# Small-window attention on quarters of the TensorE array: two heads and two query halves side by side, in place of block-diagonal k and v

## The chip, the cores and the metric

The kernel runs on one core of one Trainium2 chip. The metric is the device time of one execution in microseconds (us). The kernel before took 328.46 us in the median of four runs beside the changed one (326.58 to 329.01).

## The reference, cut to what matters

Batch 8, 8 heads, 576 positions, head dimension 64. Each head has two attentions whose results are added: a down-sampled one over 144 groups of four positions, and a local one in which position i sees only positions less than 4 away. A GELU layer pair (512 to 2048 to 512) follows on all 4608 tokens.

```python
q_d = q.reshape(B, H, Sd, 4, D).mean(axis=3)          # the same for k_d, v_d
out_d = softmax(scale * q_d @ k_d.T) @ v_d
mask = abs(pos[:, None] - pos[None, :]) < 4
out_local = softmax(where(mask, scale * q @ k.T, -1e9)) @ v
x = repeat(out_d, 4) + out_local                        # [B, H, S, D], then tokens x 512
out = gelu(x @ w_in) @ w_out
```

## The kernel before: the parts that matter

Batch 0 has its own attention and is not changed. Batches 1 to 7 run their attention between the matmuls of the two projections: `fill(n)` puts n projection matmuls (128x128 array, 512 columns each) between the steps, so that TensorE has work while ScalarE (ACT) and VectorE (DVE) compute exponentials and products. One step treats a pair of heads, p. With a head dimension of 64, two heads share the 128 rows of the array; k and v of a window are laid out block-diagonal, with zeros off the diagonal, so that each head meets only its own keys.

```python
def scores(b, p):                       # 10 windows of 57 or 60 queries, block-diagonal kb
    for hh in range(2):
        matmul(sc[:, 512*hh+SH : 512*hh+SH+Sd], lhsT=kdz[:, p, hh, 0:128], rhs=qd[:, p, :])
    for j in range(NW):
        matmul(sc[:, c : c+QL[j]], lhsT=kb[:, p, j, :], rhs=q[:, p, QN[j] : QN[j]+QL[j]])
    ...                                 # ACT: two Exp, ed (down-sampled) and e (local)

def av(b, p):
    for g in range(2):                  # sums of e, by a block matrix of ones
        matmul(sc[:, 512*g : 512*g+SH], lhsT=ON2, rhs=e[:, SH*g : SH*g+SH])
    for hh in range(2):                 # down-sampled: v and sums in one 128-column weight
        matmul(o, lhsT=vd[:, 2*p+hh, :], rhs=ed[:, hh, :], start=True, stop=False)
        matmul(o, lhsT=vlm[:, 2*p+hh, :], rhs=eL, start=False, stop=True)
    for j in range(NW):                 # windows, block-diagonal v
        matmul(nm[:, c : c+QL[j]], lhsT=vw[:, j, p, :], rhs=e[:, QN[j] : QN[j]+QL[j]])

def norm_out(b, p):                     # ACT: 1/sum as exp(-ln(sum)), local and down-sampled apart
    Ln(lr2 <- sc);  Exp(lr2);  Ln(lrd <- nm[64:128]);  Exp(lrd)
    ...                                 # DVE: xl = nm*lr2, up = nm*lrd (per head), xT = xl + up

def attn(b, fill):
    ...
    for p in range(NP):
        if p + 1 < NP: scores(b, p + 1); mask(p + 1); fill(2)
        else:          fill(4)
        av(b, p); norm_out(b, p)
        if p + 1 < NP: fill(9)
```

(Arguments shortened; sc has two buffers of two PSUM banks, nm has one.)

The softmax here doesn't subtract the row's maximum and nothing guards it: scores larger than these inputs give would overflow.

## Time and profile before

| | |
|---|---|
| time, median | 328.46 us |
| TensorE busy in the profiled execution | 317.1 of 324.5 us |
| one batch, from the third on | 32.70 us |
| of it projections: 128 matmuls of 512 columns at 0.216 | 27.65 us |
| of it attention | 5.05 us |

One batch is the distance between two starts of the first projection's first matmuls, in the chain that ended last (134.80 and 167.50, for example; read to the nanosecond in the trace, it is 32.70 in each of the five). The views that carry this are in the prediction. One more belongs here, because the change merges them: the four ACT groups of a pair's reciprocals, from the view of groups, with count, busy us and mean ns of one.

```profile
L427 ACT ACTIVATE lr<-lr 128x576 f32<-128x576 f32 x28 | 19.1, 683 | 0.9
L426 ACT ACTIVATE lr<-sc 128x576 f32<-128x576 f32 x28 | 18.4, 658 | 0.0
L429 ACT ACTIVATE lr<-lr 64x288 f32<-64x288 f32 x28 | 12.4, 443 | 0.9
L428 ACT ACTIVATE lr<-nm 64x288 f32<-64x288 f32 x28 | 11.4, 407 | 0.7
```

Together 2.19 us a pair, 61 us of ACT in all.

### The profile page before, as it was taken

To read this page: it belongs to the slowest core of one execution; us is meant where nothing else is said; L and a number is where in the kernel's file an instruction comes from. 1 tells how busy PE (TensorE), PEld (TensorE's weight loads), DVE (VectorE), ACT (ScalarE), POOL (GpSimd) and SP (SyncE) were. 2 spreads that over 40 slices of the span, in tenths; PEclk is the share of its full clock that TensorE was granted. 3 is DMA by queue.
4 is the path that set the end of the run, shared out by engine and by line. 5 is a ranking of instruction groups with operands and counts; after the bars stand their busy time and mean duration, and the time that the engine had idled before them with its cause. 6 is when DMAs were issued, how large, how long until landed. Compare 5 with 4: busy or idle time off the path is not lost.

```text
span 324.5 us, 6382 instructions
## 1 busy us (share of the span) xinstructions
PE 317.1 (98%) x2562; PEld 171.8 (53%) x2562; DVE 190.2 (59%) x410; ACT 226.7 (70%) x401; POOL 121.1 (37%) x152
## 2 busy tenths in 40 slices
PE   8899999999999999999999999999999999999995
PEld 4775556555554455445544554455445544444444
DVE  6787676667588917891789778927791750000001
ACT  8787558865887688768877787778777877415610
POOL 8965858969285155455077106200000000000000
PEclk9999999999999999999999999999999999999999
DMA  6999999999999999999999997920200020020011
GB/s 77 162 204 157 161 184 163 173 188 114 169 146 186 186 145 172 202 185 134 172 187 159 169 126 119 149 58 34 97 0 2 34 91 7 2 96 34 0 67 65
DMA packets 150974, 38.76 MB, mean 119 GB/s; under 512 B 132897, under 2 KB 146465, under 8 KB 150945
## 3 DMA queue, kind: packets, MB, share of 16 engines
q0 software_dynamic: 122256, 23.02, 90.4%
q1 hardware_dynamic: 28688, 15.34, 22.8%
q8 instruction: 20, 0.33, 0.4%
q14 instruction: 10, 0.07, 0.1%
HBM read 46.01 MB, written 15.34 MB: 189 GB/s over the span
## 4 chain that ended last, share of the span: by engine, by line
PE 92%; DMA 2%; ACT 2%; POOL 1%; DVE 1%; issue 0%; POOLq 0%; DVEq 0%
PE m_ps L282 36%; PE m_ps L251 33%; PE m_first L241 5%; PE sc L389 2%; PE nm L417 2%; DMA q_nat<-in_q_dram 2%; PE sc L407 2%; PE sc L385 1%; PE m_ps L273 1%; PE nm L413 1%; PE nm L414 1%; PE m_ps L263 1%; POOL k_nat L169 1%; PE tg_k L316 1%; PE tg_q L316 1%; PE sl L373 1%
## 5 line engine op out<-in xcount | busy, mean ns | idle before, releaser
L282 PE MATMUL m_ps<-w_out_sb,gT 128*128 128x512 f16 x544 | 127.6, 379 | 0.0
L251 PE MATMUL m_ps<-xT,w_in_sb 128*128 128x512 f16 x504 | 113.2, 379 | 0.1
L254 ACT ACTIVATE gT<-m_ps 128x512 f16<-128x512 f32 x126 | 75.2, 597 | 37.7 <-PE m_ps L251 37.7
L251 PEld LDWEIGHTS <-w_in_sb 128*128 128x128 f16 x504 | 47.9, 97 | 56.3 <-issue 1.5
L282 PEld LDWEIGHTS <-gT 128*128 128x128 f16 x544 | 49.6, 97 | 52.0 <-issue 0.3
L133 POOL DMA_DIRECT2D v_win<-in_v_dram x56 | 43.5, 812 | 29.9 <-DMA v_grp<-in_v_dram 14.8
L432 DVE TENSOR_TENSOR xl<-nm,lr 128x576 f16<-128x576 f32 x28 | 21.2, 757 | 25.4 <-ACT lr L428 25.4
L277 DVE COPY out_sb<-m_ps 128x256 f32<-128x256 f32 x2 | 0.8, 424 | 54.8 <-PE m_ps L273 54.8
L401 DVE TENSOR_TENSOR e<-e,band 128x576 f16<-128x576 f16 x28 | 12.7, 453 | 30.7 <-ACT e L396 30.7
L286 ACT COPY out_sb<-m_ps 128x512 f32<-128x512 f32 x21 | 12.3, 586 | 25.1 <-PE m_ps L282 24.9
L138 POOL DMA_DIRECT2D v_win<-in_v_dram x14 | 9.8, 787 | 34.6 <-PE nm L417 33.4
L444 DVE TENSOR_TENSOR xT<-xl,up 128x576 f16<-128x576 f16 (+8 forms) x41 | 22.1, 566 | 1.0
L427 ACT ACTIVATE lr<-lr 128x576 f32<-128x576 f32 x28 | 19.1, 683 | 0.9
L395 ACT ACTIVATE ed<-sc 128x288 f16<-128x288 f32 x28 | 11.4, 405 | 10.3 <-PE sc L389 10.3
L426 ACT ACTIVATE lr<-sc 128x576 f32<-128x576 f32 x28 | 18.4, 658 | 0.0
L396 ACT ACTIVATE e<-sc 128x576 f16<-128x576 f32 x28 | 18.0, 644 | 0.0
L434 DVE TENSOR_TENSOR up<-nm,lr 64x144 f16<-64x144 f32 x56 | 16.5, 295 | 0.4
L241 PE MATMUL m_first<-xT,w_in_sb 128*128 128x512 f16 x68 | 16.3, 379 | 0.0
L246 ACT ACTIVATE gT<-m_first 128x1024 f16<-128x1024 f32 x8 | 8.2, 1024 | 8.7 <-PE m_first L241 8.7
L156 POOL DMA_DIRECT2D q<-in_q_dram x5 | 13.8, 2766 | 0.0
L429 ACT ACTIVATE lr<-lr 64x288 f32<-64x288 f32 x28 | 12.4, 443 | 0.9
L307 DVE TENSOR_REDUCE qd<-q_nat 128x576 f16<-128x2304 f16 x5 | 12.8, 2553 | 0.2
(192 smaller groups left out, 467.8 us busy)
## 6 DMA issues: line engine op xcount, KB each, us to landing
out_dram<-out_sb SPq DMA_DIRECT2D x35, 256.0 KB, 2.7
v_win<-in_v_dram POOLq DMA_DIRECT2D x56, 72.0 KB, 7.5
v_grp<-in_v_dram POOLq DMA_DIRECT2D x7, 512.0 KB, 12.7
k<-in_k_dram POOLq DMA_DIRECT2D x5, 576.0 KB, 12.5
q<-in_q_dram POOLq DMA_DIRECT2D x5, 576.0 KB, 14.9
w_in_sb<-in_moe_w_in_dram POOLq DMA_DIRECT2D x4, 512.0 KB, 9.0
w_out_sb<-in_moe_w_out_dram POOLq DMA_DIRECT2D x4, 512.0 KB, 8.3
k_nat<-in_k_dram POOLq DMA_DIRECT2D x12, 96.0 KB, 7.4
```

What stands on the lines that cost most here:

```text
L133: nc.gpsimd.dma_start(out=vw[64 * hh:64 * hh + 64, 0:9, p, 64 * hh:64 * hh + 64], in_=bass.AP(x.tensor, x.offset, [[D, 64], [57 * D, 9], [ ...
L156: nc.gpsimd.dma_start(out=t, in_=src[b].rearrange("h s d -> s h d"))
L241: nc.tensor.matmul(out=half[j], lhsT=w_in_sb[:, fc, 128 * j:128 * j + 128], rhs=xT[:, fc, x0:x0 + 512], start=(fc == 0), stop=(fc == 3))
L251: nc.tensor.matmul(out=ps, lhsT=w_in_sb[:, fc, 128 * j:128 * j + 128], rhs=xT[:, fc, x0:x0 + 512], start=(fc == 0), stop=(fc == 3))
L254: nc.scalar.activation(out=g[:, j, :], in_=ps, func=ACTF.Gelu)
L282: nc.tensor.matmul(out=ps, lhsT=g[:, j, 128 * t:128 * t + 128], rhs=w_out_sb[:, j, :], start=(j == 0), stop=(j == NJ - 1))
L396: nc.scalar.activation(out=e.rearrange("p (g c) -> p g c", g=2), in_=sc2[:, :, 0:SH], func=ACTF.Exp, scale=0.125)
L426: nc.scalar.activation(out=lr2, in_=sc2[:, :, 0:SH], func=ACTF.Ln)
L427: nc.scalar.activation(out=lr2, in_=lr2, func=ACTF.Exp, scale=-1.0)
L432: nc.vector.tensor_tensor(out=xl.rearrange("p (g c) -> p g c", g=2), in0=nm2[:, :, 0:SH], in1=lr2, op=ALU.mult)
L434: nc.vector.tensor_tensor(out=up[64 * hh:64 * hh + 64, :], in0=nm2[0:64, hh, SH:SH + Sd], in1=lrd[:, Sd * hh:Sd * hh + Sd], op=ALU.mult)
L444: nc.vector.tensor_tensor(out=xT[:, p, y:y + z - a].rearrange("p (g r) -> p g r", r=4), in0=xl[:, a:z].rearrange("p (g r) -> p g r", r=4), ...
```

## The change

The intent: a 64-row, 64-column quarter of the array is just one head's window, so four quarters can work at once on two heads and two halves of the queries. The windows multiply and store no blocks of zeros, k needs no copy into blocks, and the sums land so that one Ln and one Exp serve both attentions.

```diff
+    def quad(fn):                       # 5 windows x 2 x 2 quarters
+        for i in range(5):
+            for a in range(2):
+                for c in range(2):
+                    fn(i, a, slice(64*a, 64*a+64), c, slice(64*c, 64*c+64), QO[i], QL[i])
     def scores(b, p):
-            matmul(sc[..], lhsT=kdz[:, p, hh, 0:128], rhs=qd[:, p, :])          # 128x128
+            matmul(sc[..], lhsT=kd[r, p, 0:128], rhs=qd[r, p, :])               # 64x128
-        for j in range(NW): ...                                                 # 10 of 128x128
+        quad(one)                                                               # 20 of 64x64
     def av(b, p):
-        for g in range(2): ... lhsT=ON2 ...                                     # 2 of 288 columns
+        for g in range(2):
+            for hh in range(2):
+                matmul(sc[hs[hh], ..SH], lhsT=ones[hs[g], :], rhs=e[hs[g], hh, :])   # 64x64
-        for hh in range(2): vd, vlm                                             # 4 of 144 columns
+        for o, own, lo in ((sc, None, m4), (nm, L["vd"], L["vlm"])):
+            for g in range(2):
+                for hh in range(2):
+                    matmul(o[hs[hh], c:c+DH], lhsT=fours or own[..], rhs=ed[:, hh, x])   # 128x64
+                matmul(o[:, c:c+DH], lhsT=lo[:, 2*p:2*p+2, :], rhs=eL[:, x])             # 128x128
-        for j in range(NW): ... lhsT=vw ...                                     # 10 of 128x128
+        quad(one)                                                               # 20 of 64x64
     def norm_out(b, p):
-        Ln, Exp on 576 columns; Ln, Exp on 288 columns of 64 partitions; up in two halves
+        Ln, Exp on 720 columns; up in one
     # v windows of batch 1: were loaded head pair by head pair, each between loads of w_out
+    # are loaded window by window, each for all eight heads
     # fills 6, 6, 2, 9, 4 become 5, 6, 2, 10, 3; warm() at the start becomes four more spins
```

(The diff is cut to its core; copies into block form and their tiles go away, and the end-of-sequence scores become four 128x32 matmuls.)

More of the change, by code (lines that the diff above doesn't have):

```diff
@@ L45 @@
     NW = 10
-    WN = [57 * i for i in range(9)] + [512]
-    QN = [0] + [57 * i + 3 for i in range(1, 10)]
-    QL = [60] + [57] * 8 + [60]
+    QL = [58, 58, 58, 57, 57]
+    QO = [0, 58, 116, 174, 231]
+    WN = [[0, 55, 113, 171, 228], [285, 343, 401, 459, 512]]
     SH = S // 2
+    DH = Sd // 2
     cpool = ctx.enter_context(tc.tile_pool(name="const", bufs=1, space=bass.MemoryType.SB))
@@ L61 @@
     I128 = cpool.tile([128, 128], F16, tag="I128", name="I128")
-    band = cpool.tile([128, S], F16, tag="band", name="band")
+    band = cpool.tile([128, 2, SH], F16, tag="band", name="band")
     BH = cpool.tile([128, 64], F16, tag="BH", name="BH")
-    ON2 = cpool.tile([128, 128], F16, tag="ON2", name="ON2")
+    ones = cpool.tile([128, 64], F16, tag="ones", name="ones")
+    fours = cpool.tile([128, 64], F16, tag="fours", name="fours")
+    m4 = cpool.tile([128, H, 64], F16, tag="m4", name="m_four")
     maskL = cpool.tile([128, H], F16, tag="maskL", name="maskL")
@@ L69 @@
     qT0 = cpool.tile([128, NP, S], F16, tag="qT", name="qT")
-    kdt = cpool.tile([128, NP, Sd], F16, tag="kdt", name="kdt")
+    kT0 = cpool.tile([128, NP, S], F16, tag="kT", name="kT")
+    kd = cpool.tile([128, NP, Sd], F16, tag="kd", name="kd")
+    KS = cpool.tile([128, NP, 32], F16, tag="KS", name="KS")
     qd = cpool.tile([128, NP, Sd], F16, tag="qd", name="qd")
-    kb = cpool.tile([128, NP, NW, 128], F16, tag="kb", name="kb")
     kdz = cpool.tile([128, NP, 2, Sd], F16, tag="kdz", name="kdz")
@@ L79 @@
             "kn": ipool.tile([128, 4096], F16, tag="kn", name="k_nat"),
-            "vw": ipool.tile([128, NW, NP, 128], F16, tag="vw", name="v_win"),
+            "vw": ipool.tile([128, 5, H, 64], F16, tag="vw", name="v_win"),
             "vt": ipool.tile([128, H, 4, 64], F16, tag="vt", name="v_grp"),
             "vl": ipool.tile([128, 4, 64], F16, tag="vl", name="v_lo"),
-            "vd": ipool.tile([128, H, 128], F16, tag="vd", name="v_d"),
+            "vd": ipool.tile([128, H, 64], F16, tag="vd", name="v_d"),
             "vls": ipool.tile([128, 64], F16, tag="vls", name="v_ls"),
-            "vlm": ipool.tile([128, H, 128], F16, tag="vlm", name="v_lm"),
+            "vlm": ipool.tile([128, H, 64], F16, tag="vlm", name="v_lm"),
         })
@@ L93 @@
     GL = cpool.tile([128, 8, 16], F16, tag="GL", name="GL")
-    four = cpool.tile([128, H], F32, tag="four", name="four")
     dum = cpool.tile([128, 2], F32, tag="dum", name="dum")
@@ L126, in load_qk, with vw_load @@
                 yield
-    def vw_load(b, src, ps=None):
-        vw = ld[b % 2]["vw"]
-        for p in ps or range(NP):
-            for hh in range(2):
-                x = src[2 * p + hh, 0:64, :]
-                nc.gpsimd.dma_start(out=vw[64 * hh:64 * hh + 64, 0:9, p, 64 * hh:64 * hh + 64],
-                                    in_=bass.AP(x.tensor, x.offset, [[D, 64], [57 * D, 9], [1, D]]))
-    def vw_last(b, src):
-        for hh in range(2):
-            nc.gpsimd.dma_start(out=ld[b % 2]["vw"][64 * hh:64 * hh + 64, 9, :, 64 * hh:64 * hh + 64],
-                                in_=src[hh:H:2, 512:576, :].rearrange("h s d -> s h d"))
+    def vw_load(b, src, i):
+        for g in range(2):
+            w = WN[g][i]
+            nc.gpsimd.dma_start(out=ld[b % 2]["vw"][64 * g:64 * g + 64, i, :, :],
+                                in_=src[:, w:w + 64, :].rearrange("h s d -> s h d"))
     def vg_load(b, src):
@@ L180 @@
     nc.scalar.activation(out=dum[:, 1:2], in_=dum[:, 0:1], func=ACTF.Exp)
-    for t in (kb.rearrange("p a j c -> p (a j c)"), ld[1]["vw"].rearrange("p j a d -> p (j a d)")):
-        nc.scalar.copy(out=t.bitcast(F32).rearrange("p (n c) -> p n c", c=256),
-                       in_=zt.bitcast(F32).unsqueeze(1).broadcast_to([128, 10, 256]))
-    nc.vector.memset(four, 4.0)
+    nc.vector.memset(ones, 1.0)
+    nc.vector.memset(fours, 4.0)
+    nc.vector.memset(KS, 0.0)
     nc.vector.memset(B0, 1.0)
@@ L288, in m2 @@
                 yield
-    def k_blocks(ps, tr):
-        for hh in range(2):
-            r = slice(64 * hh, 64 * hh + 64)
-            o = kb[r, ps, :, 64 * hh:64 * hh + 64]
-            x = tr[r]
-            nc.vector.tensor_copy(out=o[:, :, 0:9, :], in_=bass.AP(x.tensor, x.offset, [x.ap[0], x.ap[1], [57, 9], [1, 64]]))
-            nc.vector.tensor_copy(out=o[:, :, 9, :], in_=x[:, :, 512:576])
     def prep(b):
@@ L301, in prep, with k_end @@
         with nc.allow_low_precision(reason="sums of four, kept in fp16 as before"):
-            k_blocks(slice(0, NP), kt)
-            nc.vector.tensor_reduce(out=kdt, in_=kt.rearrange("p a (g r) -> p a g r", r=4), axis=AX.X, op=ALU.add)
-            for hh in range(2):
-                r = slice(64 * hh, 64 * hh + 64)
-                nc.vector.tensor_copy(out=kdz[r, :, hh, :], in_=kdt[r])
+            nc.vector.tensor_reduce(out=kd, in_=kt.rearrange("p a (g r) -> p a g r", r=4), axis=AX.X, op=ALU.add)
             nc.vector.tensor_reduce(out=qd, in_=qt.rearrange("p a (g r) -> p a g r", r=4), axis=AX.X, op=ALU.add)
-        k_lo()
+        k_end()
         v_down(b)
+    def k_end():
+        for hh in range(2):
+            r = slice(64 * hh, 64 * hh + 64)
+            nc.vector.tensor_copy(out=KS[r, :, 16 * hh:16 * hh + 16], in_=kd[r, :, 128:Sd])
     def t_in_g(b, p, which):
@@ L320, in t_in_g @@
                              rhs=Gb[0:CH, 112:136], start=True, stop=True)
-        if which == "q":
-            nc.vector.tensor_copy(out=qT0[:, p, :], in_=tr[:, 0:S])
-            nc.vector.tensor_copy(out=qd[:, p, :], in_=trf[:, 288:432])
-        else:
-            k_blocks(slice(p, p + 1), tr[:, 0:S].unsqueeze(1))
-            for hh in range(2):
-                r = slice(64 * hh, 64 * hh + 64)
-                nc.vector.tensor_copy(out=kdz[r, p, hh, :], in_=trf[r, 288:432])
+        t, d = (qT0, qd) if which == "q" else (kT0, kd)
+        nc.vector.tensor_copy(out=t[:, p, :], in_=tr[:, 0:S])
+        nc.vector.tensor_copy(out=d[:, p, :], in_=trf[:, 288:432])
     def v_down_mm(va):
@@ L353, in v_down @@
         L = ld[b % 2]
-        for x, o in ((L["vt"][:, 0:4], L["vd"][:, 0:4, 0:64]), (L["vt"][:, 4:8], L["vd"][:, 4:8, 0:64]),
+        for x, o in ((L["vt"][:, 0:4], L["vd"][:, 0:4]), (L["vt"][:, 4:8], L["vd"][:, 4:8]),
                      (L["vl"].unsqueeze(1), L["vls"].unsqueeze(1))):
             n = o.shape[1]
-            t = wpool.tile([128, S + 2 * Sd], F32, tag="lr", bufs=2, name="v_two")
+            t = wpool.tile([128, S + Sd], F32, tag="lr", bufs=2, name="v_two")
             t = t[:, 0:128 * n].rearrange("p (h r d) -> p h r d", h=n, r=2)
@@ L360, in v_down @@
             nc.vector.tensor_tensor(out=o, in0=t[:, :, 0, :], in1=t[:, :, 1, :], op=ALU.add)
-        nc.vector.tensor_tensor(out=L["vlm"][:, :, 0:64], in0=L["vls"].unsqueeze(1).broadcast_to([128, H, 64]),
+        nc.vector.tensor_tensor(out=L["vlm"], in0=L["vls"].unsqueeze(1).broadcast_to([128, H, 64]),
                                 in1=maskL.unsqueeze(2).broadcast_to([128, H, 64]), op=ALU.mult)
@@ L366, in s_lo @@
     def s_lo(b):
-        s_lo_mm(ppool.tile([128, 1024], F32, tag="nm", name="sl"))
+        tr = ppool.tile([128, 1024], F32, tag="nm", name="sl")
+        st["sl"] = tr
+        for p in range(NP):
+            nc.tensor.matmul(out=tr[32 * p:32 * p + 32, 0:Sd], lhsT=KS[:, p, :], rhs=qd[:, p, :],
+                             start=True, stop=True)
         s_lo_exp()
@@ L380, in s_lo_exp, with one @@
         st["eL"] = eL
+    def quad(fn):
+        for i in range(5):
+            for a in range(2):
+                for c in range(2):
+                    fn(i, a, slice(64 * a, 64 * a + 64), c, slice(64 * c, 64 * c + 64), QO[i], QL[i])
     def scores(b, p):
+        kt, qt = (kT0, qT0) if b <= 2 else (xT_of(b, "kn"), xT_of(b, "qn"))
         sc = ppool.tile([128, 1024], F32, tag="sc", bufs=2, name="sc")
         for hh in range(2):
-            nc.tensor.matmul(out=sc[:, 512 * hh + SH:512 * hh + SH + Sd], lhsT=kdz[:, p, hh, 0:128],
-                             rhs=qd[:, p, :], start=True, stop=True)
-        for j in range(NW):
-            c = 512 * (j // 5) + QN[j] - SH * (j // 5)
-            nc.tensor.matmul(out=sc[:, c:c + QL[j]], lhsT=kb[:, p, j, :], rhs=(qT0 if b <= 2 else xT_of(b, "qn"))[:, p, QN[j]:QN[j] + QL[j]],
-                             start=True, stop=True)
-        e = e_t[p % 3][:, 0:S]
+            r = slice(64 * hh, 64 * hh + 64)
+            nc.tensor.matmul(out=sc[:, 512 * hh + SH:512 * hh + SH + Sd], lhsT=kd[r, p, 0:128], rhs=qd[r, p, :],
+                             start=True, stop=True)
+        def one(i, hh, rh, g, rg, o, w):
+            k0, q0 = WN[g][i], SH * g + o
+            nc.tensor.matmul(out=sc[rg, 512 * hh + o:512 * hh + o + w], lhsT=kt[rh, p, k0:k0 + 64],
+                             rhs=qt[rh, p, q0:q0 + w], start=True, stop=True)
+        quad(one)
+        e = e_t[p % 3][:, 0:S].rearrange("p (a c) -> p a c", a=2)
         ed = wpool.tile([128, 2, Sd], F16, tag="ed", bufs=4, name="ed")
@@ L395, in scores @@
         nc.scalar.activation(out=ed, in_=sc2[:, :, SH:SH + Sd], func=ACTF.Exp, scale=1.0 / 128.0)
-        nc.scalar.activation(out=e.rearrange("p (g c) -> p g c", g=2), in_=sc2[:, :, 0:SH],
-                             func=ACTF.Exp, scale=0.125)
+        nc.scalar.activation(out=e, in_=sc2[:, :, 0:SH], func=ACTF.Exp, scale=0.125)
     def mask(p):
@@ L405, in av, with one @@
         e, ed, eL, sc = st[p]["e"], st[p]["ed"], st["eL"], st[p]["sc"]
-        for g in range(2):
-            nc.tensor.matmul(out=sc[:, 512 * g:512 * g + SH], lhsT=ON2, rhs=e[:, SH * g:SH * g + SH],
-                             start=True, stop=True)
         nm = ppool.tile([128, 1024], F32, tag="nm", name="nm")
         st[p]["nm"] = nm
-        for hh in range(2):
-            o = nm[:, 512 * hh + SH:512 * hh + SH + Sd]
-            nc.tensor.matmul(out=o, lhsT=L["vd"][:, 2 * p + hh, :], rhs=ed[:, hh, :], start=True, stop=False)
-            nc.tensor.matmul(out=o, lhsT=L["vlm"][:, 2 * p + hh, :], rhs=eL, start=False, stop=True)
-        for j in range(NW):
-            c = 512 * (j // 5) + QN[j] - SH * (j // 5)
-            nc.tensor.matmul(out=nm[:, c:c + QL[j]], lhsT=L["vw"][:, j, p, :], rhs=e[:, QN[j]:QN[j] + QL[j]],
-                             start=True, stop=True)
+        hs = [slice(64 * a, 64 * a + 64) for a in range(2)]
+        for g in range(2):
+            for hh in range(2):
+                nc.tensor.matmul(out=sc[hs[hh], 512 * g:512 * g + SH], lhsT=ones[hs[g], :], rhs=e[hs[g], hh, :],
+                                 start=True, stop=True)
+        for o, own, lo in ((sc, None, m4), (nm, L["vd"], L["vlm"])):
+            for g in range(2):
+                c = 512 * g + SH
+                x = slice(DH * g, DH * g + DH)
+                for hh in range(2):
+                    nc.tensor.matmul(out=o[hs[hh], c:c + DH], lhsT=fours if own is None else own[:, 2 * p + hh, :],
+                                     rhs=ed[:, hh, x], start=True, stop=False)
+                nc.tensor.matmul(out=o[:, c:c + DH], lhsT=lo[:, 2 * p:2 * p + 2, :], rhs=eL[:, x],
+                                 start=False, stop=True)
+        def one(i, g, rg, hh, rh, o, w):
+            nc.tensor.matmul(out=nm[rh, 512 * g + o:512 * g + o + w], lhsT=L["vw"][rg, i, 2 * p + hh, :],
+                             rhs=e[rg, hh, o:o + w], start=True, stop=True)
+        quad(one)
     def norm_out(b, p):
@@ L422, in norm_out @@
         nm2 = nm.rearrange("p (g c) -> p g c", c=512)
-        lr = wpool.tile([128, S + 2 * Sd], F32, tag="lr", bufs=2, name="lr")
-        lr2 = lr[:, 0:S].rearrange("p (g c) -> p g c", g=2)
-        lrd = lr[0:64, S:S + 2 * Sd]
-        nc.scalar.activation(out=lr2, in_=sc2[:, :, 0:SH], func=ACTF.Ln)
-        nc.scalar.activation(out=lr2, in_=lr2, func=ACTF.Exp, scale=-1.0)
-        nc.scalar.activation(out=lrd.rearrange("p (g c) -> p g c", g=2), in_=nm2[64:128, :, SH:SH + Sd], func=ACTF.Ln)
-        nc.scalar.activation(out=lrd, in_=lrd, func=ACTF.Exp, scale=-1.0)
+        lr = wpool.tile([128, S + Sd], F32, tag="lr", bufs=2, name="lr")
+        lr2 = lr.rearrange("p (g c) -> p g c", g=2)
+        nc.scalar.activation(out=lr2, in_=sc2[:, :, 0:SH + DH], func=ACTF.Ln)
+        nc.scalar.activation(out=lr, in_=lr, func=ACTF.Exp, scale=-1.0)
         xl = wpool.tile([128, S], F16, tag="xl", bufs=2, name="xl")
         up = wpool.tile([128, Sd], F16, tag="up", bufs=2, name="up")
-        nc.vector.tensor_tensor(out=xl.rearrange("p (g c) -> p g c", g=2), in0=nm2[:, :, 0:SH], in1=lr2, op=ALU.mult)
-        for hh in range(2):
-            nc.vector.tensor_tensor(out=up[64 * hh:64 * hh + 64, :], in0=nm2[0:64, hh, SH:SH + Sd],
-                                    in1=lrd[:, Sd * hh:Sd * hh + Sd], op=ALU.mult)
+        for t, x in ((xl, slice(0, SH)), (up, slice(SH, SH + DH))):
+            nc.vector.tensor_tensor(out=t.rearrange("p (g c) -> p g c", g=2), in0=nm2[:, :, x], in1=lr2[:, :, x], op=ALU.mult)
         x0 = S * b % XR
@@ L536, in attn @@
     def attn(b, fill):
-        fill(6)
+        fill(5)
         scores(b, 0)
@@ L547, in attn @@
             else:
-                fill(4)
+                fill(3)
             av(b, p)
@@ L553, in attn @@
             else:
-                fill(9)
+                fill(10)
     def v_load(b):
         vg_load(b, v[b])
-        vw_last(b, v[b])
-        vw_load(b, v[b])
+        for i in range(5):
+            vw_load(b, v[b], i)
     def filler(g):
@@ L577, in init @@
     def init(i):
-        if i < 2:
-            L = ld[1 - i]
-            nc.scalar.copy(out=L["vd"][:, :, 64:128], in_=four.unsqueeze(2).broadcast_to([128, H, 64]))
-            nc.scalar.activation(out=L["vlm"][:, :, 64:128], in_=maskL.unsqueeze(2).broadcast_to([128, H, 64]),
-                                 func=ACTF.Copy, scale=4.0)
-        elif i < 4:
-            t = ld[0]["vw"][:, 5 * i - 10:5 * i - 5].rearrange("p j a d -> p (j a d)")
-            nc.scalar.copy(out=t.bitcast(F32).rearrange("p (n c) -> p n c", c=256),
-                           in_=zt.bitcast(F32).unsqueeze(1).broadcast_to([128, 5, 256]))
-        elif i == 4:
-            for hh in range(2):
-                r = slice(64 * hh, 64 * hh + 64)
-                nc.vector.memset(ON2[r, 64 * hh:64 * hh + 64], 1.0)
-                nc.vector.memset(ON2[r, 64 - 64 * hh:128 - 64 * hh], 0.0)
-                nc.vector.tensor_copy(out=BH[r, :], in_=B0[r, 64 * hh:64 * hh + 64])
-        else:
-            for j in range(NW):
-                x = QN[j] - WN[j]
-                nc.vector.tensor_copy(out=band[:, QN[j]:QN[j] + QL[j]], in_=BH[:, x:x + QL[j]])
@@ L598, in warm @@
-    def warm():
-        t = ppool.tile([128, 1536], F32, tag="sc", name="warm")
-        def tiles(n, kw, mw, qs, o):
-            for i in range(n):
-                for a, b in qs:
-                    nc.tensor.matmul(out=t[b:b + mw, 512 * (a // 64) + o * (i % 4):512 * (a // 64) + o * (i % 4) + o],
-                                     lhsT=zt[a:a + kw, 0:mw], rhs=zt[a:a + kw, 0:o], start=True, stop=True)
-        tiles(4, 64, 64, ((0, 0), (0, 64), (64, 0), (64, 64)), 58)
-        tiles(4, 64, 128, ((0, 0), (64, 0)), 58)
-        tiles(2, 64, 128, ((0, 0), (64, 0)), 120)
-        tiles(4, 64, 64, ((0, 0), (64, 64)), 58)
-        tiles(1, 64, 64, ((0, 0), (0, 64), (64, 0), (64, 64)), 288)
+        if i == 0:
+            nc.scalar.activation(out=m4, in_=maskL.unsqueeze(2).broadcast_to([128, H, 64]), func=ACTF.Copy, scale=4.0)
+            return
@@ new lines, in init @@
+        if i == 1:
+            for a in range(2):
+                r = slice(64 * a, 64 * a + 64)
+                nc.vector.tensor_copy(out=BH[r, :], in_=B0[r, 64 * a:64 * a + 64])
+            return
+        for g in range(2):
+            r = slice(64 * g, 64 * g + 64)
+            for o, w, k0 in zip(QO, QL, WN[g]):
+                x = SH * g + o - k0
+                nc.vector.tensor_copy(out=band[r, 0, o:o + w], in_=BH[r, x:x + w])
+        nc.vector.tensor_copy(out=band[:, 1, :], in_=band[:, 0, :])
@@ L612 @@
     PLAN0 = """
         Rk0:D Tk0:mm0 Rq0:D Tq0:mm1 KZ10:A NB Rk1:D QD0:A KD00:D QT0:A spin2 Tk1:av Rq1:D KD10:D Tq1:mm1
-        KD01:A KZ00:A KZ01:D QT1:A spin1 S0:sc Rk3:D QD1:A Rk2:D KZ11:A Rq3:D Tk2:mm0 E10 I4 KD11:D Tk3:mm1
+        KD01:A KZ00:A KZ01:D QT1:A spin1 S0:sc Rk3:D QD1:A Rk2:D KZ11:A Rq3:D Tk2:mm0 E10 I1 KD11:D Tk3:mm1
         KD12:D E00 KZ12:D E20 I0 Tq3:av KD13:D S1:sc KZ02:A QD3:D Rq2:D KD03:A QT3:D KD02:A E11 Tq2:mm0 KL
-        VD:av E21 I1 QD2:D QT2:D E01 S2:sc VLM VDe:A KZ03:D SL:mm0 EL KZ13:D E02 spin2 AV0:av E12 NA0
@@ L617 @@
-        AV1:mm0+mm1 E22 I2 spin1 S3:sc NA1 TO0:av E13 XT0:D E23 AV2:mm0+mm1 E03 gelu NA2 TO1:av AV3:sc
-        XT1:A NA3 I5 spin1 TO2:av XT2:A I3 spin3 TO3:sc M1A XT3:D M1B
-    """
-    spin(10)
-    warm()
+        VD:av E21 QD2:D QT2:D E01 S2:sc VLM VDe:A KZ03:D SL:mm0 EL KZ13:D E02 spin2 AV0:av E12 NA0
+        AV1:mm0+mm1 E22 spin1 S3:sc NA1 TO0:av E13 XT0:D E23 AV2:mm0+mm1 E03 gelu NA2 TO1:av AV3:sc
+        XT1:A NA3 I2 spin1 TO2:av XT2:A spin3 TO3:sc M1A XT3:D M1B
+    """
+    spin(14)
@@ L720 @@
             vg_load(1, v[1])
-        elif f == 1:
-            vw_last(1, v[1])
-            vw_load(1, v[1], [0])
-        else:
-            vw_load(1, v[1], [f - 1])
-    vw_load(1, v[1], [3])
+        else:
+            vw_load(1, v[1], f - 1)
+    for i in range(3, 5):
+        vw_load(1, v[1], i)
     run(load_qk(2))
@@ L738 @@
                 f1(7 if i % 2 == 0 else 4)
-            k_lo()
+            k_end()
             v_down(b)
```

## The prediction

> **What bounds the kernel now.** I read the page first: engine shares, then the chain that ended last.
>
> ```profile
> PE 317.1 (98%) x2562; PEld 171.8 (53%) x2562; DVE 190.2 (59%) x410; ACT 226.7 (70%) x401; POOL 121.1 (37%) x152
> ...
> PE 92%; DMA 2%; ACT 2%; POOL 1%; DVE 1%; issue 0%; POOLq 0%; DVEq 0%
> ```
>
> TensorE is busy 98% of the 324.5 us, and 92% of the last chain is TensorE. A busy share of matmuls can hide pipeline slack, so I went to the timeline of TensorE inside one batch of attention (the piece for one head pair, in the batch that runs from 134.8 to 167.5 us):
>
> ```profile
> 151.74 0.29 PE L385 MATMUL sc<-qd,kdz 128*128 128x144 f16 x2
> 151.86 0.45 PE L389 MATMUL sc<-q_nat,kb 128*128 128x60 f16 x10
> 152.15 0.59 PE L282 MATMUL m_ps<-w_out_sb,gT 128*128 128x512 f16 x2
> 152.58 0.41 PE L407 MATMUL sc<-e,ON 128*128 128x288 f16 x2
> ...
> 153.08 0.45 PE L417 MATMUL nm<-e,v_win 128*128 128x60 f16 x10
> 153.37 2.10 PE L282 MATMUL m_ps<-w_out_sb,gT 128*128 128x512 f16 x9
> ```
>
> The second number of a row includes the pipeline's tail of about 0.17 us, so the cost of a group is the distance from its start to the next start. Scores of a pair: 151.74 to 152.15, 0.41 us. Sums, down-sampled part and windows: 152.58 to 153.37, 0.79 us. A 512-wide projection matmul: 0.216 (9 in 1.94). No row has an idle note: in every batch from the second on, TensorE issues without a gap, and the wait view has no entry of TensorE behind ACT or DVE after 31 us. Two windows of 32.70 us, taken from the table by stretches, both show TensorE busy 32.70, ACT 25.6 and DVE 22 to 27. So the kernel's time is the sum of TensorE's stream plus a start of about 30 us. Anything the change gives ACT, DVE or GpSimd is beside the path; only what it does to the stream counts.
>
> **What the stream says on array quarters.** The old kernel's start has a block of 40 small matmuls on zeros (warm), which happen to be the forms that the change uses: 64x64 quarters, 64x128 halves. The timeline, asked for narrow windows, gives starts:
>
> ```profile
> 4.74 0.38 PE L573 MATMUL spin<-zt 128*128 128x512 f16 x1
> ...
> 5.41 0.27 PE L604 MATMUL warm<-zt 64*128 64x120 f16 x4
> ...
> 5.61 0.37 PE L604 MATMUL warm<-zt 64*64 64x58 f16 x6
> ```
>
> and the count of matmuls in flight in successive windows:
>
> ```profile
> 5.04:5.09 0.05, 0.04 (x4) 1.00 1.11 184
> 5.09:5.12 0.03, 0.03 (x8) 1.00 0.20 34
> 5.12:5.15 0.03, 0.03 (x12) 1.00 1.94 239
> 5.15:5.18 0.03, 0.03 (x16) 1.00 1.05 171
> ```
>
> Four quarters run together: each 0.03 us window adds four matmuls of 58 columns, that is 32 ns for four, about what one full-array matmul of 57 columns costs (10 in 0.29 us, 29 ns). This is the gain the change wants.
>
> The price is in the first rows. The last full-array spin started at 4.74; streamed, it would take 0.216, yet the first quarter starts at 5.04: 0.09 us lost. Four half-array matmuls of 120 columns start at 5.41 and are streamed, two at a time, by 5.51; the first quarter after them starts at 5.61: 0.10 lost, though there only the columns of the tile changed (64x128 to 64x64). The same shows in batch 0, where one matmul has 60 rows:
>
> ```profile
> 23.96 0.37 PE L521 MATMUL av<-I,nall 116*128 116x116 f16 x4
> 24.26 0.20 PE L523 MATMUL av<-I,nall 60*128 60x60 f16 x1
> 24.39 0.20 PE L525 MATMUL av<-U,nall 128*128 128x64 f16 x1
> 24.43 0.20 PE L526 MATMUL av<-I,nall 124*128 124x64 f16 x1
> ```
>
> Four of about 113 columns take 0.19 to 0.20, so 24.26 is 0.10 late; 60 columns take 0.03, so 24.39 is 0.10 late; 24.39 to 24.43 is normal again. Every change of tile shape costs 0.09 to 0.10 us of TensorE, in and out, with no wait noted by the profile. I use 97 ns, and 15 ns more where small matmuls follow (the first group after a change took some 50 ns in place of 32).
>
> **The Trainium skill.** "TensorEngine Tiling (Array Packing)", Tiling Modes, Key Properties: "Changing tiling mode (not just tile) drains the TensorE", and tiles work independently. This trace agrees with both (0.10 us, and 32 ns for four). "TensorE: Matmul & The Clock Gate", Back-to-back issue gap, gives N/2.4 + 2.5 ns isolated, and a smaller sustained figure, 131 ns, at 512; the trace shows 216 ns, the isolated one, and I take the trace. Restrictions and Gotchas of the tiling page forbid different row tiles in the same PSUM bank at once; the diff puts row halves in different banks, so I expect no loss there.
>
> **The change part by part, TensorE, for one head pair** (28 of them: 7 batches, 4 pairs).
>
> *Scores.* Before: 2 of 144 and 10 of 57 columns, 0.41. After: 2 of 64x128, 144 columns, on different row halves, together 62 ns; 20 quarters in 5 groups of 32 = 160 ns; three changes of shape (128x128 to 64x128, to 64x64, back) 3 x 97 = 291; some 33 for first groups. Sum 546. Difference +0.13.
>
> *Sums, down-sampled part, windows.* Before 0.79. After: 4 quarters of 288 columns together 122; then, for two tiles and two halves, a pair of 128x64 matmuls of 72 columns (34) and one 128x128 of 72 columns (30), 4 x 64 = 256; 20 quarters 160. Streaming: 538, some 0.25 less than before. But the shapes alternate: in (1), to 128x64 (1), four times to 128x128 and three times back (7), to 64x64 (1), out (1): 11 changes, 1067. With 54 for first groups: 1.66. Difference +0.87.
>
> Sum +1.00 us a pair, 28.0 us in all. Once a batch the end-of-sequence scores go from 0.25 (four of 144) to 62 + one more change = 0.16: 7 x -0.09 = -0.6.
>
> *Start.* ACT loses two fills of v_d and v_lm and four zero fills; v_d and v_lm lie on the chain for about 1.0 us near 18 us, but TensorE's next step there also waits for its own v sums until 19.0, so I count -0.3. The removed warm block (1.0 us) is replaced by four more spins (0.86), and both lie before a wait for loaded k.
>
> *ACT* per pair: two Ln and two Exp (658 + 683 + 407 + 443 ns) become one each at 720 columns. From the two lengths, (658-407)/288 = 0.87 ns a column, so about 783 + 810; some 0.6 us less. *DVE*: no window copies of k, no copies to kdz, one multiply for up in place of two at 295. Perhaps 4 us a batch less. All of it beside a gapless TensorE: worth 0. *DMA*: the window loads carry the same rows in 10 larger transfers in place of 10 smaller; queue 0 is 90% busy, but a slower TensorE only gives it more time.
>
> Sum: 328.5 + 28.0 - 0.6 - 0.3 = 355.6; I say 355.
>
> **Rivals.**
> 1. *Only the number of rows matters: 128x64 and 128x128 alternate freely.* Then 7 of the 11 changes vanish: 7 x 97 x 28 = 19 us less, 336.5 us. For it: no 128x64 form is in the trace. Against: the 64x128 to 64x64 change is one of columns alone and cost 0.10.
> 2. *The array hides the changes*, because weight loads are pulled ahead behind 512-wide matmuls. Then the streaming saving counts: (0.41 + 0.79 - 0.22 - 0.54) x 28 = 12, with 1 for the ends: 315 us. Against: the spin before warm was 512 wide, and 0.09 was lost.
> 3. *A gain from ACT and DVE*, which are lighter: nothing unless TensorE waits for them, and it does not: within 1 us of 328.
> 4. *A new wait*: nm has one buffer, and its reader is now one Ln, one Exp, and two multiplies. That chain gets shorter (about 2.7 in place of 2.8 us) while the time between two pairs grows by 1 us. No.
>
> **Range and chances.** The main case (80%) puts the cost of a change between 85 and 110 ns: 399 changes by 25 ns is 10 us wide, so 350 to 360. Rival 1 (some 13%) lies at 336, still over 2% slower. Between them are mixtures (some changes partly hidden by in-order tails). I take 344 to 361. Faster needs rival 2: 3%. Within 2%: 4%.
>
> **What would show it.** In the timeline of a pair: scores 0.55 us, from first sums to the next projection 1.66, with gaps of about 0.10 between rows of different shape and no releaser; batches of 36.5 us instead of 32.7. Quarters groups at 32 ns for four. ACT busy down by some 20 us with its idle up. Wrong if the 72-column rows follow each other at 30 ns (rival 1), if quarters do not run together (a group of 20 then takes over 0.5 us, and the time passes 361), or if TensorE waits for ACT, DVE or a DMA anywhere after 31 us.

## The result

The changed kernel took 362.78 us in the median of four runs (359.67 to 363.75): slower, ratio 1.1041 with a 95% interval of 1.0974 to 1.1109. The prediction was 355 with a range of 344 to 361: right in direction and mechanism, but the median lies 1.8 us outside the range. Forecast were 26.5 us more, measured 34.3.

The page of the changed kernel, busy shares and the chain by engine:

```profile
PE 350.5 (98%) x3366; PEld 179.3 (50%) x3366; DVE 164.6 (46%) x319; ACT 204.5 (57%) x338; POOL 118.2 (33%) x152
...
PE 87%; DMA 7%; POOL 3%; DVE 2%; issue 1%; POOLq 0%; DVEq 0%
```

TensorE is still busy 98% of the span, with 33 us more of it; ACT lost 22 us and DVE 26, and the time went up all the same. New is 7% of DMA in the chain (2% before): 16.3 us of it are one load of w_out and then windows of v, 37.12 to 48.75 and 49.99 to 54.70, just before the first pair of batch 1 goes on. The last experiments come back to it. The two ACT groups that replace the four, from the view of groups:

```profile
L430 ACT ACTIVATE lr<-lr 128x720 f32<-128x720 f32 x28 | 22.5, 802 | 0.9
L429 ACT ACTIVATE lr<-sc 128x720 f32<-128x720 f32 x28 | 21.6, 772 | 13.1 <-PE sc L416 13.1
```

They take 1.57 us a pair in place of 2.19, about as estimated (783 + 810 ns), and before the Ln (L429, the first of the two in time) ACT now idles 13.1 us in all for TensorE. Making an engine faster that TensorE does not wait for bought nothing.

Where the time went is in TensorE's timeline of one pair (start us, us with the pipeline's tail, then line and form); the rows answer to those of the kernel before in the prediction:

```profile
167.22 0.24 PE L380 MATMUL sc<-qd,kd 64*128 64x144 f16 x2
167.39 0.35 PE L385 MATMUL sc<-q_nat,k_nat 64*64 64x58 f16 x20
167.67 0.60 PE L277 MATMUL m_ps<-w_out_sb,gT 128*128 128x512 f16 x2
168.21 0.32 PE L407 MATMUL sc<-e,ones 64*64 64x288 f16 x4
168.45 0.22 PE L414 MATMUL sc<-ed,fours 128*64 128x72 f16 x2
168.61 0.21 PE L416 MATMUL sc<-eL,m_four 128*128 128x72 f16 x1
168.74 0.22 PE L414 MATMUL sc<-ed,fours 128*64 128x72 f16 x2
168.90 0.21 PE L416 MATMUL sc<-eL,m_four 128*128 128x72 f16 x1
...
169.48 0.21 PE L416 MATMUL nm<-eL,v_lm 128*128 128x72 f16 x1
169.62 0.35 PE L420 MATMUL nm<-e,v_win 64*64 64x58 f16 x20
169.90 0.39 PE L277 MATMUL m_ps<-w_out_sb,gT 128*128 128x512 f16 x1
```

Twenty quarters take 0.28 us with the change behind them (167.39 to 167.67): 52 ns for the first group, four more at 32, and the rest is the next change. So the quarters do run four at a time. But two 128x64 matmuls of 72 columns, which stream in 0.03 us, hold TensorE for 0.16 (168.45 to 168.61), and one 128x128 of 72 columns, also 0.03 of streaming, holds it for 0.13 to 0.14. No row has an idle note: TensorE is called busy while the array changes its shape. From the first sums (168.21) to the projection (169.90) it is 1.70 us to the nanosecond, and with the 0.09 that is lost before 168.21, 1.79, where it was 0.79.

The weight loads (PEld) show more of it. In the kernel before, the load for the sums starts at 152.37, while the matmul before them still streams; they start at 152.58. In the changed kernel the load for the sums starts at 168.20 and the sums at 168.21: across a change of shape the weights did not come ahead. The view of waits notes this for two changes of each pair, those that leave the projection, and the kernel before has no such entry ("issue" means that the profile shows nothing waited for; of each 0.4 us, 0.12 are there before too, 0.22 are the last projection matmul, and 0.09 are the loss):

```profile
PEld L407 <- issue: 11.9, 28, 0.4
PEld L380 <- issue: 11.4, 27, 0.4
```

One batch is now 37.26 us (150.33 to 187.60), 4.57 more. With 14 changes of shape in each of four pairs and one more for the end-of-sequence scores, a batch has 57. Streaming by itself became shorter: (0.41 + 0.79 - 0.222 - 0.538) x 4 and 0.19 for the end of the sequence are 1.95 us. So 57 changes cost 6.5 us, 0.114 us each in the mean, with the slower first matmuls after a change counted in. Seven batches make 32.0 of the 34.3 us.

### The profile page after: what moved, and what is told of

It reads as the page before. It is cut to its first block, busy times and chain, and to the rows that moved or that the text cites. A ratio compares the mean times of both kernels' runs of the same rounds, so it can differ in the third digit from the quotient of the medians.

```text
span 358.0 us, 7871 instructions
## 1 busy us (share of the span) xinstructions
PE 350.5 (98%) x3366; PEld 179.3 (50%) x3366; DVE 164.6 (46%) x319; ACT 204.5 (57%) x338; POOL 118.2 (33%) x152
## 4 chain that ended last, share of the span: by engine, by line
PE 87%; DMA 7%; POOL 3%; DVE 2%; issue 1%; POOLq 0%; DVEq 0%
PE m_ps L277 34%; PE m_ps L246 27%; PE m_first L236 4%; DMA w_out_sb<-in_moe_w_out_dram 3%; PE nm L414 2%; PE sc L414 2%; DMA q_nat<-in_q_dram 2%; PE nm L420 2%; PE nm L416 2%; PE sc L416 2%; PE sc L385 2%; PE sc L407 2%; DMA v_win<-in_v_dram 1%; PE sc L380 1%; PE m_ps L268 1%
## 5 line engine op out<-in xcount | busy, mean ns | idle before, releaser
L134 POOL DMA_DIRECT2D v_win<-in_v_dram x70 | 48.8, 770 | 95.6 <-PE nm L420 75.9
L429 ACT ACTIVATE lr<-sc 128x720 f32<-128x720 f32 x28 | 21.6, 772 | 13.1 <-PE sc L416 13.1
L430 ACT ACTIVATE lr<-lr 128x720 f32<-128x720 f32 x28 | 22.5, 802 | 0.9
L236 PE MATMUL m_first<-xT,w_in_sb 128*128 128x512 f16 x68 | 16.3, 379 | 0.0
L289 DVE TENSOR_REDUCE kd<-k_nat 128x576 f16<-128x2304 f16 x5 | 12.7, 2546 | 0.0
L414 PE MATMUL sc<-ed,fours 128*64 128x72 f16 x112 | 12.5, 220 | 0.0
L414 PE MATMUL nm<-ed,v_d 128*64 128x72 f16 x112 | 12.5, 220 | 0.0
```

Source lines behind the costliest of these rows:

```text
L134: nc.gpsimd.dma_start(out=ld[b % 2]["vw"][64 * g:64 * g + 64, i, :, :], in_=src[:, w:w + 64, :].rearrange("h s d -> s h d"))
L236: nc.tensor.matmul(out=half[j], lhsT=w_in_sb[:, fc, 128 * j:128 * j + 128], rhs=xT[:, fc, x0:x0 + 512], start=(fc == 0), stop=(fc == 3))
L414: nc.tensor.matmul(out=o[hs[hh], c:c + DH], lhsT=fours if own is None else own[:, 2 * p + hh, :], rhs=ed[:, hh, x], start=True, stop=False)
L429: nc.scalar.activation(out=lr2, in_=sc2[:, :, 0:SH + DH], func=ACTF.Ln)
L430: nc.scalar.activation(out=lr, in_=lr, func=ACTF.Exp, scale=-1.0)
```

## The experiments

**Theory 1**: the number of changes of the array's shape sets the loss, 0.114 us each, whatever kind. **Rival A**: loading weights of 64 columns is slow in itself. **Rival B**: the loss is in waits and at the start. Later, for the last 2 us, **theory 2**: the windows of v of batch 1 come too late; **rival C**: they don't matter. All outputs are right. "Batch" is the steady length, from the third batch on (in e3 and e6 from the fourth).

| run | changes a batch | batch, us | median, us | ratio to before |
|---|---|---|---|---|
| kernel before | 0 | 32.70 | 327.85 (same rounds as e1 to e4) | 1 |
| changed kernel | 57 | 37.26 | 362.78 | 1.1041 |
| e1_grouped | 33 | 34.53 | 344.02 | 1.0490 |
| e2_order | 25 | 33.61 | 337.81 | 1.0304 |
| e3_merged | 19 | 33.10 | 339.61 | 1.0348 |
| e4_hybrid | 10 | 32.98 | 338.22 | 1.0282 |
| d1_quarters | 8 | 33.73 | 334.97 | 1.0214 |
| d2_columns | 8 | 33.73 | 336.23 | 1.0241 |
| d3_full | 0 | 32.96 | 328.81 | 1.0022 |

### e1_grouped: the same matmuls, grouped by shape

```diff
-        for o, own, lo in (...):
-            for g in range(2):
-                two of 128x64;  one of 128x128
+        for every (o, g): two of 128x64
+        for every (o, g): one of 128x128
```

> The changed kernel with one thing moved: in the second half of a pair all eight 128x64 matmuls come first and the four 128x128 ones after them, so a batch has 33 changes of tile shape in place of 57; the number of matmuls and of weight loads is the same. Theory 1 (each change of shape costs some 0.114 us, which is what 32.0 us more over seven batches plus 13.5 us of saved streaming make of 399 changes): 24 x 7 x 0.114 = 19 us less than the changed kernel, about 343 us. Rival A (weight loads of 64 columns are slow by themselves, whatever stands next to them): no change, 360 to 364 us. Rival B (the time goes at start and in waits of ACT or DMA): no change either.

Measured 344.02 us (343.58 to 345.85). The batch fell by 2.73 us for 24 changes less: 0.114 each. The same weights are loaded as often as before, so rival A falls, and so does B for this part.

### e2_order: fewer changes still

```diff
-        sums (64x64); 128x64; 128x128; windows (64x64)
+        sums (64x64); windows (64x64); 128x64; 128x128      # and the projection, 128x128
```

> As the run before, and the window quarters are moved up next to the sums of quarters, so the order of shapes in the second half is 64x64, 128x64, 128x128 and then the projection, which is 128x128 too: 25 changes a batch in place of 57. Theory 1: 32 x 7 x 0.114 = 25.5 us less than the changed kernel, about 337 us. Rivals A and B: 360 to 364 us.

Measured 337.81 us (337.12 to 339.19). Another 0.92 us a batch for 8 changes: 0.115. The timeline of one pair shows what the grouped rows now cost:

```profile
160.39 0.32 PE L411 MATMUL nm<-e,v_win 64*64 64x58 f16 x20
160.64 0.26 PE L418 MATMUL sc<-ed,fours 128*64 128x72 f16 x4
160.73 0.23 PE L418 MATMUL nm<-ed,v_d 128*64 128x72 f16 x4
160.89 0.24 PE L421 MATMUL sc<-eL,m_four 128*128 128x72 f16 x2
160.97 0.23 PE L421 MATMUL nm<-eL,v_lm 128*128 128x72 f16 x2
161.03 0.38 PE L277 MATMUL m_ps<-w_out_sb,gT 128*128 128x512 f16 x1
```

Eight 128x64 matmuls and the change behind them take 0.25 us (160.64 to 160.89), against four times 0.16 when the shapes alternated. The last four, 128x128, take 0.14 and need no change to get back to the projection.

### d1_quarters, d2_columns, d3_full: the cost of a change by itself

Into the kernel *before*, in each of the 28 pairs, between projection and sums, goes a piece of work on zeros whose result nobody reads:

```diff
     def av(b, p):
+        # d1: four 64x64 matmuls of 58 columns, into unused columns of sc
+        # d2: two 128x64 matmuls of 72 columns
+        # d3: two 128x128 matmuls of 72 columns
         sums, down-sampled part, windows as before
```

> The kernel before with four extra 64x64 matmuls of 58 columns on zeros in every pair, between the projection and the sums; their result goes to unused PSUM columns. It measures one change to quarters and back by itself. Theory 1: 93 in, 53 of streaming with the first group's delay, 102 out, 10 for the next: 0.25 us a pair, 28 pairs, 7 us more than the kernel before: 335.5 us. If changes of shape were free, 28 x 0.03 = 1 us more.

> The same with two extra matmuls of 128 rows by 64 columns, 72 columns of data, on the two column halves: only the number of columns changes. Theory 1 with the larger exit that the changed kernel shows: 100 in, 34 of streaming, 126 out, 10: 0.27 us a pair, 7.5 us more: 336 us, slightly more than for quarters. If changes of columns alone were free: 1 us more.

> The control: the same place, two extra full-array matmuls of 72 columns, no change of shape. All theories: 2 x 30 ns a pair, 1.7 us more than the kernel before: about 330 us.

Measured: d1 334.97 us (334.28 to 335.53), d2 336.23 (334.94 to 336.80), d3 328.81 (328.08 to 328.97), with 327.74 for the kernel before in the same rounds. The verdict on d1 and d2 against the 2% line is "unclear" and their intervals are wide (d1 1.0147 to 1.0281), but the batch lengths repeat within 0.005 us. d1: 33.73 - 32.70 = 1.03, a quarter of it is 0.258 a pair; less 0.032 of streaming, two changes cost 0.226, 0.113 each. d2: 0.259 a pair, less 0.034: again 0.113 each. d3: 0.26 a batch, 0.066 a pair, nearly all streaming. The rows of d1:

```profile
157.25 0.22 PE L408 MATMUL sc<-zt 64*64 64x58 f16 x4
157.40 0.42 PE L411 MATMUL sc<-e,ON 128*128 128x288 f16 x2
```

and those of d2:

```profile
158.63 0.22 PE L407 MATMUL sc<-zt 128*64 128x72 f16 x2
158.79 0.42 PE L410 MATMUL sc<-e,ON 128*128 128x288 f16 x2
```

In d1 the full array comes back 0.15 us after the quarters started, in d2 0.16. A change of columns alone costs as much as one of rows and columns, so rival 1 of the prediction (128x64 and 128x128 alternate freely) is wrong. And one more rival falls: in the changed kernel each 128x128 matmul adds to what the two 128x64 before it wrote, and a wait for these sums would look alike; in d2 nothing is added to and the loss is the same.

### e3_merged and e4_hybrid: can quarters win at all?

```diff
     # e3: as e2, and
-            scores(b, p + 1); mask(p + 1); fill(2); av(b, p); norm_out(b, p); fill(10)
+            scores(b, p + 1); mask(p + 1);          av(b, p); norm_out(b, p); fill(12)
     # e4: as e3, and the down-sampled part, its end-of-sequence scores and norm_out
     #     are those of the kernel before (128x128, zero-padded kdz, two Ln and two Exp)
```

> As the run before, and the scores of the next pair stand directly before the second half of this pair, with no projection matmuls between them, so that they share one stretch of quarters: 19 changes a batch. Theory 1: 38 x 7 x 0.114 = 30 us less than the changed kernel, about 332 us, within 1 or 2% of the kernel before. Rivals A and B: 360 to 364 us. If moving the two projection matmuls opened a wait for ACT, TensorE would show idle there and the time would be above 335.

> Quarters only where they save streaming (scores, sums and windows, in one shared stretch a pair), the down-sampled part in the full array as in the kernel before, with its zero-padded k and its two Ln and two Exp: 10 changes of shape a batch. Theory 1: per batch 10 x 0.114 = 1.1 us of changes against 4 x (0.13 + 0.12 + 0.13) = 1.5 us of saved streaming, 2.7 us less than the kernel before over seven batches: about 326 us, faster than both. If the start of the changed kernel is slower by itself (1 to 2 us), 327 to 328. Rivals A and B give no number for it, but a time of 340 or more would speak for A.

Measured: e3 339.61 us (339.25 to 340.31), e4 338.22 (334.66 to 340.25, of which the 340.25 was a slow run; the five fast ones alone have 338.01). Both misses, by some 8 and 12 us, for two reasons.

First, the steady batch. e3 has 33.10 where 33.61 - 6 x 0.114 = 32.93 was due, e4 32.98 where 32.70 - 0.4 = 32.3 was due. In a batch's first merged pair of both the sums start 0.15 us late, right after DVE's mask product of e has ended (e3: 197.13 and 197.18); for e3 that is nearly all. e4 has one wait more, in its timeline of one pair:

```profile
167.26 0.30 PE L403 MATMUL sc<-e,ones 64*64 64x288 f16 x4
167.68 0.35 PE L407 MATMUL nm<-e,v_win 64*64 64x58 f16 x20
167.96 0.24 PE L412 MATMUL nm<-ed,v_d 128*128 128x144 f16 x1
```

The windows start 0.42 us after the sums, 0.30 more than the 0.12 that the sums stream: nm has one buffer, and its reader was late. The trace shows the wait, though TensorE's row has no note: the view of waits has the weight loads of the windows waiting for DVE's product up, which reads nm (PEld L407 <- DVE up L429: 3.1 us in 12 waits), and in one batch they cost 0.30 and 0.16 us. With the 0.15 that is 0.61 of the 0.68 us missing. Why the reader is late, the ACT timeline suggests: with scores and sums ready together, both Exp of the next pair (1.05 us) stand between the sums and the first Ln of this one. No run with another order tested that. It is the wait that the prediction's rival 4 ruled out; for the changed kernel that was right, for e4's tighter schedule it is not.

Second, the first batches. In e3 batch 1 took 47.83 us and in e4 47.23 (36.34 in the kernel before), with waits of TensorE for the windows of v (4.0 and 1.7 us) and one for an output copy (2.2 and 2.9 us). That led to theory 2.

### a1_again, e5_vhalves, e6_order_vhalves, e7_hybrid_vhalves: the windows of batch 1

```diff
     # v windows of batch 1, among the loads of w_out
-            window 0, 1, .. 4: all eight heads
+            window 0 .. 4: heads 0 to 3;  later window 0 .. 4: heads 4 to 7
```

> The changed kernel again, unaltered, so that the next runs have it in the same rounds. All theories: 360 to 364 us.

> The changed kernel with one thing altered: the v windows of batch 1 are loaded for heads 0 to 3 first and for heads 4 to 7 later, between the same loads of w_out, so that the first pair of batch 1 needs half of the bytes; same bytes in all. Theory 2 (what the changes of shape leave unexplained, 34.3 - 32.0 = 2.3 us, is TensorE waiting for the windows of batch 1, which the change loads for all heads at once, and the lower clock after that wait): the wait of 0.5 us on the windows is gone, the mean clock is nearer to 1.0, and the time falls by 1.5 to 3 us, to about 360.5. Rival C (the rest lies in batch 0 and in chance of the clock there): no change.

> The run with 25 changes of shape a batch, with the same split loads. There batch 1 took 41.4 us where 37.3 (36.34 + 0.92) follows from its later batches, so theory 2 has 3 to 4 us to win: about 334 us. Rival C: no change, 337.8.

> The kernel with the full array for the down-sampled part and 10 changes of shape a batch, with the split loads. Its batch 1 took 47.2 us in place of 36.6, which is 10.6 us; some of it is not the windows (a wait of 3.3 us for an output copy near 63 us). Theory 2: 5 to 8 us less than 338.2, 330 to 333; its later batches take 32.98 against 32.69 of the kernel before, because of waits on the one nm buffer, so it can't beat the kernel before by more than noise. Rival C: no change.

Measured, all beside 328.0 us for the kernel before (12 runs, one of them slow): a1 361.42 us (360.37 to 363.57), e5 358.68 (357.67 to 359.80), e6 335.46 (335.06 to 338.20), e7 333.73 (331.98 to 334.67). So the split loads win 2.7 us on the changed kernel, 2.4 on e2 and 4.5 on e4. (The comparisons of e6 with e2 and of e7 with e4 are across rounds; the kernel before differs by 0.15 us between them.) For e6 the gain is 1 us short of what was expected (TensorE still waits 1.2 us for a window, and 1.4 us for w_out), and e7 missed its range by 0.7 us. Rival C falls; theory 2 stands for e5 with a limit: of the 2.7 us the traces show 1.3 in batch 1. The rest they do not place; the granted clocks of the runs, 0.990 to 0.995 in a1 and 0.995 to 1.000 in e5, fit the clock part of the theory, but clocks also scatter without it (see the start, below).

In the first pair of batch 1, the windows' rows of a1:

```profile
53.97 1.23 PE L420 MATMUL nm<-e,v_win 64*64 64x58 f16 x18
55.42 0.21 PE L420 MATMUL nm<-e,v_win 64*64 64x57 f16 x2 [0.21 <-DMA v_win<-in_v_dram]
55.56 0.82 PE L258 MATMUL m_ps<-w_out_sb,gT 128*128 128x512 f16 x3
```

and of e5:

```profile
53.57 0.35 PE L420 MATMUL nm<-e,v_win 64*64 64x58 f16 x20
53.85 0.82 PE L258 MATMUL m_ps<-w_out_sb,gT 128*128 128x512 f16 x3
```

From the windows to the projection it is 1.59 us in a1 and 0.28 in e5. Only 0.21 of the difference is noted as idle in TensorE's rows; the rest is hidden because each small matmul's row reaches over 0.19 us and the late windows came one after the other. The view of waits of the weight loads has 1.0 us, in four waits, for the same windows. Batch 1 took 42.06 us in a1 and 40.75 in e5, and 36.34 + 4.57 = 40.91 is what the changes of shape alone ask for. The kernel before had loaded the windows pair by pair, so its first pair needed a quarter of them.

Where TensorE waited longer, its granted clock was lower as well. In e1 the first pair of batch 1 waited 1.89 us in one piece, up to 52.90; from the table by stretches (window, its length, TensorE, weight loads, DVE, ACT, POOL, granted clock, DMA):

```profile
50.00:55.00 5.00, 2.30 (x35) 1.28 (x34) 0.46 (x1) 2.14 (x4) 3.69 (x5) 0.73 1.88 138
55.00:60.00 5.00, 4.80 (x35) 1.89 (x36) 1.73 (x3) 0.00 (x0) 5.00 (x8) 0.59 1.94 123
```

The clock was 0.73 and 0.59 in these ten microseconds; in a1, with 0.21 us noted as idle, it was 1.00 from 48 to 72. From the windows to the projection it is 4.63 us in e1 (50.76 to 55.39), 4.35 more than in e5. The nine projection matmuls after that took 3.77 us (55.39 to 59.16) in place of 9 x 0.216 = 1.94, 1.83 more. Together that is 6.2 us, against the 6.0 us by which e1's batch 1 (44.19) exceeds 36.34 + 1.84. That the wait made the clock fall fits, but no run tested it.

None of the versions beats the kernel before. e7 comes nearest, at 1.0165; it still waits 2.9 us in batch 1 for an output copy on DVE, and its steady batch is 0.29 us longer.

## Why the prediction was wrong, point by point

- *The bound.* Right. TensorE's stream sets the time; 22 us less of ACT and 26 us less of DVE are worth nothing.
- *Quarters run four at a time at 32 ns.* Right: 21 to 22 ns after the last of a group starts the next, 32 to 33 from group to group.
- *A change of columns alone costs as much.* Right, by d2, and so rival 1 falls. Rival 2 falls: entering from 512-wide matmuls still cost 93 ns. Rival 3 falls with the bound.
- *The step that failed: the sum of the second half, "11 changes, 1067. With 54 for first groups: 1.66".* The mechanism was right; this term was too small. Scores came out as predicted, 0.546 us (167.12, where the projection's 0.216 end, to 167.67). The second half took 1.79: less 0.538 of streaming and 1.067 for eleven changes at 97 ns, 0.185 are left where 0.054 had been entered. The prediction's own rule, "15 ns more where small matmuls follow", asked for more: six of the eleven changes lead to quarters or 128x64 matmuls, which is 90 ns, and four to 128x128 matmuls of only 72 columns, which makes 150. The rows show both parts. Leaving a 512-wide matmul cost 93 to 96 ns, leaving small ones 102 to 104 (in e2 from the last two 128x64 matmuls to the first 128x128, 134 from start to start, less 30). And the first group after a change takes some 20 ns longer than the next: quarters 52 and 32, in e2 two 128x64 matmuls 52 and 32. The missing 131 ns by 28 pairs are 3.7 us of the 4.6 us (32.0 - 27.4) by which the forecast for the changes fell short. Put as a mean, the sum had 0.103 us a change and the runs gave 0.113 to 0.115 (e1, e2, d1, d2). My case for the range, 85 to 110 ns, did not reach that.
- *"DMA: ... a slower TensorE only gives it more time"*: failed in batch 1. I counted bytes and transfers, not which of them the first pair needs. All windows were now due before the first pair's, and TensorE waited 0.7 us (profiled execution) to 1.3 us (a1); undoing half of it in e5 won 2.7 us, of which the traces show 1.3 there.
- *Start, -0.3 us*: too small to be seen. The first projection of batch 0 began at 30.82 us in the profiled execution, 1.15 later than before, and TensorE's clock was 0.87 and 0.70 between 12 and 20 us, against 1.00 in the profile before. But the kept traces scatter by more: with the start of the kernel before it began at 29.67, 30.20, 31.13 and 32.68 (before, d3, d1, d2), in the nine traces of changed versions between 28.51 (e1) and 31.04 (a1). The clock from 12 to 20 us was 0.79 in d1, d2, the changed kernel, a1, e2 and e5 and 1.00 in the others, so the slower clock comes and goes with either start.

Together, of the 34.3 us: 32.0 for the changes net of streaming, where 27.4 was forecast; 0.7 to 1.3 for the wait in batch 1; the rest, 1.0 to 1.6, is of the size of this scatter and is not placed further.

## What to carry to other kernels

Count changes of array shape, not matmuls: here each change, rows or columns, in or out, cost TensorE 0.114 us in the mean with no idle shown in its rows, so a stretch of small tiles has to save over 0.23 us of streaming to pay for entering and leaving, and work of one shape belongs together. Changing only the order of the same matmuls won 25 us here. And when loads are regrouped, ask which bytes the first consumer needs, not how many bytes there are.

## What the Trainium skill lacked or had wrong

- "TensorEngine Tiling (Array Packing)", Key Properties: it says that a change of mode drains TensorE, but not how long. Measured 0.114 us in the mean with the slower first group after it; the change alone 0.093 when a 512-wide matmul is left and 0.104 when 128x64 matmuls of 72 columns are (e2).
- The same page lists 128x64 and 128x128 as configurations, but does not say whether going from one to the other, with all rows in both, is such a change. It is: 0.113 us (d2).
- "TensorE: Matmul & The Clock Gate", Part 3: its span of a packed group, one matmul plus some 4 ns a tile, agrees with the starts of 3 to 4 ns apart here, but it has no term for entering and leaving, 0.226 us for a group of four that streams in 0.032 (d1).
- The same page, Back-to-back issue gap, gives 131 ns as the sustained spacing at 512 columns. The traces here have 0.216 us between the projection's matmuls at full clock.
- That TensorE's rows can show the time of a change of shape, or of matmuls that wait one by one, as busy: "Perfetto Trace Analysis" says that TensorE's end times are estimated and that its busy share is a bad measure of how close a kernel is to its limit, but names neither case. a1's windows lost 1.3 us, of which 0.21 was noted as idle there and 1.0 in the waits of the weight loads.
